# The last 128 rows of w2, four to a partition on 32 partitions, in a decode step of attention and a Mish layer

## The chip, the cores and the metric

The kernel runs on one core of a Trainium2 chip. The metric is device time in microseconds of one execution, the median of several; lower is better. All data is float32.

## The reference

Two branches work on the same input x (2 rows of 512) and are mixed by a gate. Branch A is one decode step of attention: 32 query heads over 8 key/value heads of width 128, a cache of which the last 4096 positions count, softmax, and an output projection wo. Branch B is a dense layer w1 (512 to 1792), Mish, and a dense layer w2 (1792 to 512).

```python
g = sigmoid((x * gate_w).sum(-1, keepdims=True))
q = (x @ wq) in heads                       # 32 heads of 128
p = softmax(q @ k^T * 128**-0.5)            # k, v: the last 4096 positions
a = (p @ v) in rows @ wo                    # [2, 4096] @ [4096, 512]
h = x @ w1 + b1                             # [2, 1792]
b = (h * tanh(softplus(h))) @ w2            # [2, 1792] @ [1792, 512]
return g * a + (1 - g) * b
```

## The kernel before

All weights and the cache are read once, 91 MB in all, by DMAs that the SP queue issues in the order of the code. Big loads go through a pool of five buffers (`stream`, L46 and L54 to L57): a load is issued when the buffer that it reuses is free. The order is wq (two loads, with the small vector `sm` between them), w1, then k and v of the eight key/value heads in turn, then `w2_0` (the first ten blocks of 128 rows of w2, L270), then wo in four pieces of 4, 2, 1 and 1 key/value heads (L271, here called wo0, wo4, wo6 and wo7), and at last the rest of w2 in pieces of two, one and one blocks (L272; `CUTS`, L39; here called w2_10, w2_12 and w2_13). The three last pieces have buffers of their own (pool `ends`), so they wait for nothing but their turn on SP. Each load fills all 128 partitions, and each partition's part is one run of memory.

Early on, `queries` (L112) projects x with wq, and `hidden` (L207) computes the Mish layer up to `actT`, whose column block f holds 128 activations of w2's row block f; (1 - g) is folded in. `hidden` brings four groups of 32 output rows from PSUM through ACT (L218, L219), transposes them with four TensorE transposes (L228), adds the bias on DVE (L232), and does the rest on POOL, ACT and DVE (L237 to L245).

Then for each key/value head come `softmax` (L131) and `values` (L150). After the last head, `outputs` (L199) puts the heads' results into `oT`.

The last matmuls are of two kinds. `project` (L278, matmul at L279) adds a product with 512 columns into one of four groups of 32 rows of `acc`; four of them, one a group, run beside each other. It takes the ten blocks of `w2_0` and the 32 heads of wo. When all of `acc` is there, ACT copies its first half and DVE its second half into `asum` (L307, L308). `finish` (L287, matmul at L289) adds products of four times 128 columns into the four groups of `fin`: `output(1)` for w2_10, then `asum` against `fold`, which adds up the four groups of `acc`, then `output(2)` for w2_12 and `output(3)` for w2_13. DVE copies `fin` (L320) and SP stores it (L321).

The framework orders each engine's instructions by its own estimate of when operands arrive; in the trace the last `outputs` (L201) runs ahead of the ten blocks of `w2_0`, though the code has it behind them. A float32 matmul is two instructions in the trace (each with its weight load), so that four matmuls, one for each group, are eight.

Of the kernel before, what the change touches and what calls it, by code (L numbers as in the profile page):

```python
# [8 lines left out]
F32 = mybir.dt.float32  # L9
AF = mybir.ActivationFunctionType  # L10
ALU = mybir.AluOpType
AX = mybir.AxisListType

P = 128
B = 2
D = 512
HQ = 32
HKV = 8
REP = HQ // HKV
# [5 lines left out]
NJ = 4  # L25
NT = 4
Q = 32
RS = Q // B
BH = B * REP
F = 1792  # L30
DC = D // P
FC = F // P
FG = 4
HALF = 4
CHUNK = 8192
SMALL = DC * B + DC + FC
SCALE = DH ** -0.5
CAP = 20.0
CUTS = (0, 10, 12, 13, 14)  # L39


@with_exitstack
def decode_kernel(ctx: ExitStack, tc: tile.TileContext, res, stored, small, wq, kt, v, wo, w1, w2, out):
    nc = tc.nc

    stream = ctx.enter_context(tc.tile_pool(name="stream", bufs=5))  # L46
    ends = ctx.enter_context(tc.tile_pool(name="ends", bufs=1))
# [39 lines left out]
    nc.gpsimd.memset(qz, 0.0)  # L87
    oT = const.tile([P, HQ, Q], F32, name="oT")
    nc.gpsimd.memset(oT, 0.0)
    actT = const.tile([P, FC, Q], F32, name="actT")  # L90
    nc.gpsimd.memset(actT, 0.0)
    mx = const.tile([P, HKV], F32, name="mx")
    ls = const.tile([P, HKV], F32, name="ls")
# [113 lines left out]
    def hidden(t):  # L207
        w = t[:, : DC * F].rearrange("p (c f) -> p c f", c=DC)
        hp = ps_1.tile([P, FG * P], F32, tag="o", name="hp")
        for c in range(DC):  # L210
            for j in range(NJ):
                n = min(FG, FC - j * FG) * P
                nc.tensor.matmul(hp[Q * j : Q * j + Q, :n], x32[:, c, :],  # L213
                                 w[:, c, j * FG * P : j * FG * P + n],
                                 start=(c == 0), stop=(c == DC - 1))
        hs = work.tile([P, FG * P], F32, tag="p", name="hs")
        nl = (FC - (NJ - 1) * FG) * P
        nc.scalar.copy(hs[:, :nl], hp[:, :nl])  # L218
        nc.scalar.copy(hs[: Q * (NJ - 1), nl:], hp[: Q * (NJ - 1), nl:])  # L219
        ht = ps_1.tile([P, FG, NJ, Q], F32, tag="pt", name="ht")  # L220

        def m(name):
            return const.tile([P, FC, B], F32, name=name)

        h, e, nu, de, ho = (m(x) for x in ("h", "e", "nu", "de", "ho"))
        for k in range(FG):
            nj = len(range(k, FC, FG))
            nc.tensor.transpose(ht[:, k, :nj, :].rearrange("p j r -> p (j r)"),  # L228
                                hs[: Q * nj, k * P : (k + 1) * P], ident[: Q * nj, : Q * nj])
        for j0, j1, nk in ((0, NJ - 1, FG), (NJ - 1, NJ, FC - (NJ - 1) * FG)):  # L230
            f0, f1 = j0 * FG, (j1 - 1) * FG + nk
            nc.vector.tensor_tensor(  # L232
                h[:, f0:f1, :].rearrange("p (j k) b -> p j k b", k=nk),
                ht[:, :nk, j0:j1, ::RS].rearrange("p k j b -> p j k b"),
                b1[:, f0:f1].rearrange("p (j k) -> p j k", k=nk)[:, :, :, None]
                .to_broadcast([P, j1 - j0, nk, B]), op=ALU.add)
        nc.gpsimd.tensor_scalar_min(e, h, CAP)  # L237
        nc.scalar.activation(e, e, AF.Exp)
        nc.gpsimd.tensor_tensor(ho, h, omg[:, None, :].to_broadcast([P, FC, B]), op=ALU.mult)
        nc.gpsimd.tensor_scalar_add(nu, e, 2.0)  # L240
        nc.gpsimd.tensor_tensor(nu, nu, e, op=ALU.mult)
        nc.gpsimd.tensor_scalar_add(de, nu, 2.0)
        nc.vector.reciprocal(de, de)
        nc.gpsimd.tensor_tensor(nu, nu, de, op=ALU.mult)
        nc.gpsimd.tensor_tensor(actT[:, :, ::RS], nu, ho, op=ALU.mult)  # L245
# [11 lines left out]
    def load_w2(i):  # L257
        f0, f1 = CUTS[i], CUTS[i + 1]
        src = w2[f0 * P * D : f1 * P * D].rearrange("(p x) -> p x", p=P)
        if i == 0:  # L260
            return load(src, (f1 - f0) * D, f"w2_{f0}")
        t = ends.tile([P, (f1 - f0) * D], F32, name=f"w2_{f0}")
        nc.sync.dma_start(t, src)
        return t

    def load_wo(k0, k1):
        return load(wo[k0 * REP * D * P : k1 * REP * D * P].rearrange("(p x) -> p x", p=P),
                    (k1 - k0) * REP * D, f"wo{k0}")

    w2_0 = load_w2(0)  # L270
    wos = [(k0, k1, load_wo(k0, k1)) for k0, k1 in ((0, 4), (4, 6), (6, 7), (7, 8))]  # L271
    tail = [load_w2(i) for i in range(1, len(CUTS) - 1)]  # L272

# [4 lines left out]
    def project(j, lhsT, rhs, n):  # L278
        nc.tensor.matmul(acc[Q * j : Q * j + Q, :], lhsT, rhs,  # L279
                         start=(n_col[j] == 0), stop=(n_col[j] == n - 1))  # L280
        n_col[j] += 1

    n_of = [HKV + len(range(j, CUTS[1], NJ)) for j in range(NJ)]
    n_fin = FC - CUTS[1] + 1
    done = [0]

    def finish(lhsT, rhs):  # L287
# [9 lines left out]
    values(HKV - 1, pT, last_v)  # L297
    for f in range(CUTS[1]):
        project(f % NJ, actT[:, f, :], w2_0[:, f * D : (f + 1) * D], n_of[f % NJ])
    outputs(ol, kf, r, HKV - 2, HKV)  # L300
    for k0, k1, t in wos:
        for kv in range(k0, k1):
# [7 lines left out]
    def output(i):  # L310
        for f in range(CUTS[i], CUTS[i + 1]):
            x = (f - CUTS[i]) * D
            finish(actT[:, f, :], tail[i - 1][:, x : x + D])
# [1 line left out]
    output(1)  # L315
    finish(fold, asum)
    output(2)
    output(3)

    copy = nc.vector.tensor_copy(res, fin)  # L320
    store = nc.sync.dma_start(out, res).then_inc(stored, 16)  # L321
# [51 lines left out]
```

## Time and profile before

| | |
|---|---|
| time, median of 3 runs | 219.93 us (219.87 to 219.94) |
| the profiled execution's own time | 219.96 us |
| its span, first to last instruction | 218.1 us |
| mean granted TensorE clock | 0.82 of full speed |
| read from memory, rate over the span | 91.24 MB, 419 GB/s |
| busy: PE, PEld, DVE, ACT, POOL | 128.1, 39.7, 22.1, 15.3, 7.5 us |

Between the span and the time of the same execution lie 1.86 us. Times within the profile are microseconds from the span's start. PE is the matmul side of TensorE, PEld its weight loads; SPq is SP's queue, from which the DMAs are issued. A DMA's share of 1.00 means that all 16 DMA engines of the core are at work.

### The profile page before, as it was taken

To read this page: it belongs to the slowest core of one execution; us is meant where nothing else is said; L and a number is where in the kernel's file an instruction comes from. 1 tells how busy PE (TensorE), PEld (TensorE's weight loads), DVE (VectorE), ACT (ScalarE), POOL (GpSimd) and SP (SyncE) were. 2 spreads that over 40 slices of the span, in tenths; PEclk is the share of its full clock that TensorE was granted. 3 is DMA by queue.
4 is the path that set the end of the run, shared out by engine and by line. 5 is a ranking of instruction groups with operands and counts; after the bars stand their busy time and mean duration, and the time that the engine had idled before them with its cause. 6 is when DMAs were issued, how large, how long until landed. Compare 5 with 4: busy or idle time off the path is not lost.

```text
span 218.1 us, 1832 instructions
## 1 busy us (share of the span) xinstructions
PE 128.1 (59%) x804; PEld 39.7 (18%) x804; DVE 22.1 (10%) x34; ACT 15.3 (7%) x34; POOL 7.5 (3%) x29
## 2 busy tenths in 40 slices
PE   0059855275565619555571944477293837593995
PEld 0023221012111202111120211112021212432222
DVE  0000000010001230100105010010501002105001
ACT  2000111001002000200200020011002001100000
POOL 7000002000000000000000000000000000100000
PEclk9999999578859985797967599676969797557599
DMA  7998999999999999999999999999999999999992
GB/s 288 409 459 385 452 413 472 391 475 403 463 415 451 412 451 415 451 415 451 421 442 427 433 433 439 427 439 424 439 427 445 421 445 404 436 449 427 406 408 109
DMA packets 4182, 91.41 MB, mean 419 GB/s; under 512 B 592, under 2 KB 720, under 8 KB 1104
## 3 DMA queue, kind: packets, MB, share of 16 engines
q1 hardware_dynamic: 4176, 91.31, 97.6%
q8 instruction: 6, 0.10, 0.2%
HBM read 91.24 MB, written 0.07 MB: 419 GB/s over the span
## 4 chain that ended last, share of the span: by engine, by line
DMA 82%; PE 14%; DVE 1%; SPq 1%; issue 1%; ACT 1%; POOL 0%; POOLq 0%
DMA k<-in_kt 41%; DMA w<-in_w 21%; DMA v<-in_v 19%; PE sc L135 5%; PE o L156 4%; PE hp L213 2%; PE ol L201 1%; PE fin L289 1%; SPq L56 1%; ACT p L140 0%; DVE mx L138 0%; PE lp L192 0%; POOL ms L180 0%; DVE r L195 0%; SPq L61 0%
## 5 line engine op out<-in xcount | busy, mean ns | idle before, releaser
L135 PE MATMUL sc<-k,qz 128*32 128x512 f32 x256 | 46.0, 885 | 40.1 <-DMA k<-in_kt 40.1
L156 PE MATMUL o<-v,pT 128*32 128x512 f32 x256 | 39.2, 768 | 11.4 <-DMA v<-in_v 11.4
L135 PEld LDWEIGHTS sc<-k,qz 128*32 128x32 f32 x256 | 10.3, 154 | 74.5 <-DMA k<-in_kt 46.7
L156 PEld LDWEIGHTS o<-v,pT 128*32 128x32 f32 x256 | 10.9, 136 | 34.1 <-issue 28.2
L138 DVE TENSOR_REDUCE mx<-sc 128x1 f32<-128x512 f32 x8 | 5.5, 692 | 107.1 <-PE sc L135 107.1
L117 PE MATMUL qp<-wqa,x 128*32 128x512 f32 x32 | 8.0, 953 | 13.4 <-POOL x L85 13.4
L140 ACT ACTIVATE p<-sc,mx 128x512 f32<-128x512 f32 x8 | 5.5, 687 | 131.8 <-DVE mx L138 131.8
L144 PE MATMUL pp<-ident,p 128*128 128x128 f32 x32 | 5.3, 287 | 12.1 <-ACT p L140 12.1
L279 PE MATMUL acc<-wo,oT 128*32 128x512 f32 x64 | 8.7, 616 | 0.4 <-DMA wo<-in_wo 0.4
L163 DVE TENSOR_TENSOR om<-o,pick 128x1024 f32<-128x1024 f32 x4 | 4.9, 1224 | 29.0 <-PE o L156 29.0
L166 DVE TENSOR_REDUCE od<-om 128x256 f32<-128x1024 f32 x4 | 7.5, 1884 | 0.1
L144 PEld LDWEIGHTS pp<-ident,p 128*128 128x128 f32 x32 | 3.4, 141 | 19.1 <-ACT p L140 19.1
L201 PE MATMUL ol<-kf,od 128*128 128x8 f32 x16 | 3.8, 364 | 3.9 <-DVE od L166 3.3
L180 POOL TENSOR_TENSOR ms<-ms,top 8x64 f32<-8x64 f32 x2 | 0.6, 310 | 146.4 <-DVE top L178 146.4
L145 ACT COPY pT<-pp 128x512 f32<-128x512 f32 x8 | 4.7, 586 | 6.2 <-PE pp L144 6.2
L279 PE MATMUL acc<-w,actT 128*32 128x512 f32 x20 | 5.1, 1037 | 0.0
L213 PE MATMUL hp<-w,x 128*32 128x512 f32 (+1 forms) x32 | 3.6, 542 | 1.9 <-DMA w<-in_w 1.9
L117 PEld LDWEIGHTS qp<-wqa,x 128*32 128x32 f32 x32 | 1.5, 157 | 17.3 <-POOL x L85 13.4
L201 PEld LDWEIGHTS ol<-kf,od 128*128 128x128 f32 x16 | 3.6, 328 | 5.0 <-DVE od L166 4.2
L117 PE MATMUL qp<-wqb,x 128*32 128x512 f32 x32 | 3.6, 595 | 0.0
L279 PEld LDWEIGHTS acc<-wo,oT 128*32 128x32 f32 x64 | 2.2, 113 | 5.9 <-issue 4.7
L307 ACT COPY asum<-acc 128x256 f32<-128x256 f32 x1 | 0.4, 372 | 27.7 <-PE acc L279 27.7
(67 smaller groups left out, 33.0 us busy)
## 6 DMA issues: line engine op xcount, KB each, us to landing
k<-in_kt SPq DMA_DIRECT2D x8, 4096.0 KB, 43.1
v<-in_v SPq DMA_DIRECT2D x8, 4096.0 KB, 42.6
wqa<-in_wq SPq DMA_DIRECT2D x1, 4096.0 KB, 12.2
wqb<-in_wq SPq DMA_DIRECT2D x1, 4096.0 KB, 21.1
wo<-in_wo SPq DMA_DIRECT2D x1, 4096.0 KB, 39.3
w<-in_w SPq DMA_DIRECT2D x1, 3584.0 KB, 29.1
w<-in_w SPq DMA_DIRECT2D x1, 2560.0 KB, 39.5
wo<-in_wo SPq DMA_DIRECT2D x1, 2048.0 KB, 34.4
```

What stands on the lines that cost most here:

```text
L117: nc.tensor.matmul(qp[Q * k : Q * k + Q, :], x32[:, c, :], w[:, c, k, :], start=(c == 0), stop=(c == DC - 1))
L135: nc.tensor.matmul(sc[Q * j : Q * j + Q, :], qz[:, kv, m * Q : m * Q + Q], t[:, (m * NJ + j) * 512 : (m * NJ + j + 1) * 512], start=(m == ...
L138: nc.vector.tensor_reduce(mx[:, kv : kv + 1], sc, axis=AX.X, op=ALU.max, negate=True)
L140: nc.scalar.activation(p, sc, AF.Exp, bias=mx[:, kv : kv + 1], accum_out=ls[:, kv : kv + 1])
L144: nc.tensor.transpose(pp[:, c, :], p[:, c * P : (c + 1) * P], ident)
L145: nc.scalar.copy(pT, pp)
L156: nc.tensor.matmul(o[Q * j : Q * j + Q], pT[:, c, Q * j : Q * j + Q], t[:, (c * NJ + j) * 512 : (c * NJ + j + 1) * 512], start=(c == 0), s ...
L163: nc.vector.tensor_tensor(ov, pair[0].rearrange("p k (m d) -> p k m d", m=BN), pick[:, None, :, None].to_broadcast([P, 2, BN, DH]), op=ALU ...
L166: nc.vector.tensor_reduce(od[:, kv - 1 : kv + 1], ov.rearrange("p k m d -> p k d m"), axis=AX.X, op=ALU.add)
L201: nc.tensor.matmul(ol[:, kv].rearrange("p b h -> p (b h)"), od[:, kv, :], kf[:, kv, :], start=True, stop=True)
L213: nc.tensor.matmul(hp[Q * j : Q * j + Q, :n], x32[:, c, :], w[:, c, j * FG * P : j * FG * P + n], start=(c == 0), stop=(c == DC - 1))
L279: nc.tensor.matmul(acc[Q * j : Q * j + Q, :], lhsT, rhs, start=(n_col[j] == 0), stop=(n_col[j] == n - 1))
```

## The change

The 14th block of w2 (rows 1664 to 1791) leaves the tail. It is laid out as four rows of w2 per partition on partitions 0 to 31, 8 KB a partition (`w2_x`), and loaded right behind `w2_0` by four DMAs, the i-th of which fills partitions i, i+4, ..., i+28. It is used by four matmuls with 32 rows instead of 128, one for each group of `acc`, placed behind the ten blocks of `w2_0`; `output(3)` is gone. For these matmuls the last 128 activations must lie as four columns of 32 partitions: `hidden` gets four more transposes of 32 columns each, into a PSUM tile `hx` of their own, one more bias add, and a memset of `h`; `actT` and the Mish tiles grow from 14 to 17 columns. The vector `sm` grows by three columns.

```diff
+FM = FC - 1
+NX = P // Q
+FA = FM + NX
-SMALL = DC * B + DC + FC
+SMALL = DC * B + DC + FA
-CUTS = (0, 10, 12, 13, 14)
+CUTS = (0, 10, 12, 13)
...
-    actT = const.tile([P, FC, Q], F32, name="actT")
+    actT = const.tile([P, FA, Q], F32, name="actT")
...
-            return const.tile([P, FC, B], F32, name=name)
+            return const.tile([P, FA, B], F32, name=name)
...
         for k in range(FG):
-            nj = len(range(k, FC, FG))
+            nj = len(range(k, FM, FG))
             nc.tensor.transpose(ht[:, k, :nj, :].rearrange("p j r -> p (j r)"),
                                 hs[: Q * nj, k * P : (k + 1) * P], ident[: Q * nj, : Q * nj])
-        for j0, j1, nk in ((0, NJ - 1, FG), (NJ - 1, NJ, FC - (NJ - 1) * FG)):
+        jx, kx = FM // FG, FM % FG
+        hx = ps_1.tile([P, NX, NJ, Q], F32, tag="q", name="hx")
+        for q in range(NX):
+            nc.tensor.transpose(hx[:Q, q].rearrange("p j r -> p (j r)"),
+                                hs[:, kx * P + q * Q : kx * P + (q + 1) * Q], ident)
+        nc.gpsimd.memset(h, 0.0)
+        nc.vector.tensor_tensor(h[:Q, FM:, :], hx[:Q, :, jx, ::RS],
+                                b1[:Q, FM:, None].to_broadcast([Q, NX, B]), op=ALU.add)
+        for j0, j1, nk in ((0, NJ - 1, FG), (NJ - 1, NJ, FM - (NJ - 1) * FG)):
...
     w2_0 = load_w2(0)
+    w2_x = ends.tile([P, NX * D], F32, name="w2_x")
+    for i in range(REP):
+        nc.sync.dma_start(w2_x[i:Q:REP, :], w2x[i])
     wos = [(k0, k1, load_wo(k0, k1)) for k0, k1 in ((0, 4), (4, 6), (6, 7), (7, 8))]
...
-    n_of = [HKV + len(range(j, CUTS[1], NJ)) for j in range(NJ)]
-    n_fin = FC - CUTS[1] + 1
+    n_of = [HKV + len(range(j, CUTS[1], NJ)) + 1 for j in range(NJ)]
+    n_fin = FM - CUTS[1] + 1
...
     for f in range(CUTS[1]):
         project(f % NJ, actT[:, f, :], w2_0[:, f * D : (f + 1) * D], n_of[f % NJ])
+    for q in range(NX):
+        project(q, actT[:Q, FM + q, :], w2_x[:Q, q * D : (q + 1) * D], n_of[q])
     outputs(ol, kf, r, HKV - 2, HKV)
...
     finish(fold, asum)
     output(2)
-    output(3)
...
+    w2x = a("B_w2")[FM * P :].reshape(NX, Q // REP, REP, D).transpose(2, 1, 0, 3)
```

## Rows read from the trace of the kernel before

**Rows 1.** The page: DMA share and rate in forty slices, and the chain's shares.

```profile
DMA  7998999999999999999999999999999999999992
GB/s 288 409 459 385 452 413 472 391 475 403 463 415 451 412 451 415 451 415 451 421 442 427 433 433 439 427 439 424 439 427 445 421 445 404 436 449 427 406 408 109
DMA 82%; PE 14%; DVE 1%; SPq 1%; issue 1%; ACT 1%; POOL 0%; POOLq 0%
```

**Rows 2.** The chain that ended last, its end: start, length, what.

```profile
197.84 16.40 DMA w<-in_w
...
214.29 1.78 PE fin L289 x40
...
216.09 0.29 DVE res L320
```

**Rows 3.** The timeline of the tail: start, length, instruction, idle time before it.

```profile
213.07 1.06 PE L279 MATMUL acc<-wo,oT 128*32 128x512 f32 x8 [0.36 <-DMA wo<-in_wo]
214.21 0.37 ACT L307 COPY asum<-acc 128x256 f32<-128x256 f32 x1 [27.67 <-PE acc L279]
...
214.29 0.65 PE L289 MATMUL fin<-w,actT 128*32 128x128 f32 x16
214.61 0.42 DVE L308 COPY asum<-acc 128x256 f32<-128x256 f32 x1 [12.70 <-ACT asum L307]
...
215.10 0.30 PE L289 MATMUL fin<-w,actT 128*32 128x128 f32 x2
...
215.24 0.79 PE L289 MATMUL fin<-w,actT 128*32 128x128 f32 x14
```

**Rows 4.** The busy times by stretch, around the end of the DMAs.

```profile
core 0: us, PE busy (x) PEld busy (x) DVE busy (x) ACT busy (x) POOL busy (x), PEclk, DMA share, GB/s
...
213.00:213.20 0.20, 0.13 (x4) 0.13 (x8) 0.00 (x0) 0.00 (x0) 0.00 (x0) 1.00 1.03 410
...
213.60:214.00 0.40, 0.40 (x8) 0.00 (x0) 0.00 (x0) 0.00 (x0) 0.00 (x0) 1.00 0.38 149
...
214.60:214.80 0.20, 0.20 (x15) 0.20 (x8) 0.19 (x1) 0.00 (x0) 0.00 (x0) 1.00 0.34 133
...
215.00:215.20 0.20, 0.20 (x8) 0.11 (x8) 0.04 (x1) 0.00 (x0) 0.00 (x0) 1.00 0.11 41
```

**Rows 5.** The page: DMA queues and kinds, with packets, MB and share.

```profile
q1 hardware_dynamic: 4176, 91.31, 97.6%
q8 instruction: 6, 0.10, 0.2%
```

**Rows 6.** The timeline of SP's queue: the last loads before the store.

```profile
154.01 0.33 SPq L56 DMA_DIRECT2D w<-in_w  x1
...
197.84 1.37 SPq L263 DMA_DIRECT2D w<-in_w  x3
```

**Rows 7.** The issue and landing of the loads at L263.

```profile
L263 SPq DMA_DIRECT2D w<-in_w x3: 423/427/432, 197.8 to 198.8; - x3
DMA to landing us min/median/max: 16.4/16.6/16.8
```

**Rows 8.** The busy times by stretch, from the last head's values to wo7.

```profile
197.40:200.60 3.20, 0.00 (x0) 0.00 (x0) 3.10 (x2) 0.00 (x0) 0.00 (x0) 0.83 1.07 461
200.60:206.30 5.70, 5.63 (x28) 2.08 (x30) 0.20 (x2) 0.00 (x0) 0.00 (x0) 0.50 0.93 398
206.30:212.70 6.40, 6.40 (x56) 1.71 (x50) 0.00 (x0) 0.00 (x0) 0.00 (x0) 1.00 0.99 413
```

**Rows 9.** The timeline of TensorE between the last outputs and wo7.

```profile
200.67 1.02 PE L201 MATMUL ol<-kf,od 128*128 128x8 f32 x4 [3.28 <-DVE od L166]
...
201.62 4.48 PE L279 MATMUL acc<-w,actT 128*32 128x512 f32 x18
...
202.48 0.20 PEld L279 LDWEIGHTS acc<-w,actT 128*32 128x32 f32 x4 [0.66 <-issue]
203.33 0.20 PEld L279 LDWEIGHTS acc<-w,actT 128*32 128x32 f32 x4 [0.66 <-issue]
...
206.54 0.15 PEld L279 LDWEIGHTS acc<-wo,oT 128*32 128x32 f32 x6 [0.47 <-issue]
...
207.40 0.15 PEld L279 LDWEIGHTS acc<-wo,oT 128*32 128x32 f32 x6 [0.32 <-issue]
```

**Rows 10.** The instructions of L279 that read wo: shortest, median, longest in ns.

```profile
L279 PE MATMUL acc<-wo,oT x64: 592/592/1062, 205.0 to 213.5; 128*32 128x512 f32 x64
```

**Rows 11.** The timeline around the Mish layer, and POOL's next work after it.

```profile
35.51 0.65 PE L228 MATMUL ht<-ident,hs 128*128 128x128 f32 x4 [0.55 <-ACT hs L218]
...
38.92 0.25 POOL L245 TENSOR_TENSOR actT<-nu,ho 128x28 f32<-128x28 f32 x1
...
42.42 3.63 PE L135 MATMUL sc<-k,qz 128*32 128x512 f32 x16 [6.25 <-DMA k<-in_kt]
...
185.61 0.59 POOL L180 TENSOR_TENSOR ms<-ms,top 8x64 f32<-8x64 f32 x2 [146.44 <-DVE top L178]
```

**Rows 12.** The page: the issue of w2_0, KB, us to landing.

```profile
w<-in_w SPq DMA_DIRECT2D x1, 2560.0 KB, 39.5
```

More of the change, by code (lines that the diff above doesn't have):

```diff
@@ L33, with decode_kernel @@
 FG = 4
+FM = FC - 1
+NX = P // Q
+FA = FM + NX
 HALF = 4
 CHUNK = 8192
-SMALL = DC * B + DC + FC
+SMALL = DC * B + DC + FA
 SCALE = DH ** -0.5
 CAP = 20.0
-CUTS = (0, 10, 12, 13, 14)
+CUTS = (0, 10, 12, 13)
 @with_exitstack
-def decode_kernel(ctx: ExitStack, tc: tile.TileContext, res, stored, small, wq, kt, v, wo, w1, w2, out):
+def decode_kernel(ctx: ExitStack, tc: tile.TileContext, res, stored, small, wq, kt, v, wo, w1, w2, w2x, out):
     nc = tc.nc
@@ L238, in hidden @@
         nc.scalar.activation(e, e, AF.Exp)
-        nc.gpsimd.tensor_tensor(ho, h, omg[:, None, :].to_broadcast([P, FC, B]), op=ALU.mult)
+        nc.gpsimd.tensor_tensor(ho, h, omg[:, None, :].to_broadcast([P, FA, B]), op=ALU.mult)
         nc.gpsimd.tensor_scalar_add(nu, e, 2.0)
@@ L337 @@
     x = a("A_x")[:, 0, :]
+    b1 = a("B_b1")
     small = np.concatenate([
@@ L340 @@
         a("gate_w").reshape(DC, P).T,
-        a("B_b1").reshape(FC, P).T,
+        b1[: FM * P].reshape(FM, P).T,
+        np.concatenate([b1[FM * P :].reshape(NX, Q).T, np.zeros((P - Q, NX), b1.dtype)]),
     ], axis=1)
@@ L358 @@
         "w2": c(w2),
+        "w2x": c(w2x.reshape(REP, Q // REP, NX * D)),
     }
```

## The prediction

> **What bounds the kernel now.** I read the page's slices and chain first. All but the first and the last slices have the DMA engines busy nine tenths or more of the time, and DMAs make up 82% of the chain that ended last [rows 1]. So the stream of loads sets the pace, and since the change reads the same bytes, only its end can move: what lands last, and what must still run after that. For this the end of the chain, then the timeline of the tail.
>
> The chain's last DMA is w2_10: issued at 197.84, landed 16.40 later at 214.24. Then `fin` takes 1.78 us and DVE copies the result from 216.09 [rows 2]. The timeline shows a second line beside it. wo7's eight instructions start at 213.07, on their DMA's landing, and run 1.06 us. ACT's half of `asum` starts at 214.21, DVE's at 214.61 and ends at 215.03. The `fin` work behind it starts at 215.10, and the last of it ends at 216.03 [rows 3]. w2_13 is issued last of the three at L263; 198.8 and the longest landing, 16.8, give 215.6 [rows 7]. So three things end close together: w2_10 at 214.24, `asum` at 215.03, w2_13 at about 215.6.
>
> The stretches show how the loads run out. The DMA share is 1.03 up to 213.2, then 0.38 at 213.6 to 214.0, 0.34 at 214.6 and 0.11 at 215.0 [rows 4]. A share of 0.38 is six engines of sixteen: ten are done at about 213.5, six work on for some 1.3 us. The page shows six packets of kind "instruction", 0.10 MB in all, 16 KB each [rows 5]. Six late engines and six such packets: I read each fetch as having put one engine, a different one each time, behind the rest. The trace doesn't number the engines; whether they are among those that the change loads more is the question on which the forecast hangs.
>
> **The change, part by part.**
>
> *Taken from the tail.* w2_13's eight `fin` instructions go. What is then last is `asum`: DVE ends at 215.03 and `fin` goes on at 215.10. The four groups' passes follow each other at 0.117 us (sixteen instructions in 0.65, the first 0.30 long, so three steps in 0.35). Left are two passes of the second half of `fold` and two of w2_12: 215.10 + 3 x 0.117 + 0.30 = 215.75 instead of 216.03 [rows 3]. Gain: 0.28, taken as 0.3. That w2_13's landing moves from 215.6 gives no more than this, because `asum` doesn't move with it.
>
> *Added to TensorE.* Four matmuls of 512 columns, eight instructions. No row has one with 32 rows and 512 columns; the nearest are the same shape with 128 rows. Eight of these take 0.86 at the full clock (207.40 less 206.54) and 1.70 at half (203.33 less 202.48 is 0.85 for four) [rows 9]. The ends are nothing, if the four run in an idle time, and 1.70. They need `w2_x`, which follows `w2_0`, and the trace has the blocks of `w2_0` behind the last `outputs` at 201.62 [rows 9], although TensorE idles from 197.4 to 200.6 [rows 8]. I assume the same order. [...] The clock rises at its time, so the price is a round at the full clock, 0.86. Of this the idle time before wo7 takes 0.36 [rows 3], and the pipelined end another 0.16: a pass is shown 592 ns long [rows 10], but the next starts 0.43 after it. 0.86 - 0.52 = 0.34. So wo7 starts about 0.3 later than 213.07, and with it `asum` and the end. Cost: 0.3.
>
> *Moved among the loads.* 256 KB that were last now come ahead of wo0, wo4, wo6, wo7, w2_10 and w2_12, and the bytes in front of each are 256 KB more. At 413 GB/s [rows 8] this is 0.63 us if all engines share it evenly. Do they? 4176 packets on the loads' queue [rows 5] are 29 DMAs (28 loads and the store) of 128 rows and 16 more each, so a row is a packet, and a DMA of eight rows can use eight engines at most. Four such DMAs of 8 KB rows put 32 KB on each if they all go to the same eight: at 413/16 = 25.8 GB/s an engine, 1.25 us for these and none for the others. The ten engines that are early have 1.3 us to spare, so loads on them land no later than the late six do now. So the landing of wo7 stays if the eight are clear of the six, and moves by 1.25 if any of the six is among them.
>
> [...]
>
> *Costed at nothing.* The Mish layer's four more transposes, its memset, its bias add and its wider tiles: the whole of L228 to L245 takes from 35.51 to 39.17, TensorE's next work waits for k until 42.42 [rows 11], and `actT` isn't used before 201.62. Four transposes now take 0.65, so four more fit five times into the gap of TensorE. POOL has nothing else to do until 185.61 [rows 11], and DVE's next reduction waits for TensorE. Without this cover they would cost about 1 us: 0.65 of transposes and some 0.3 for the bias add. SP's four more issues take 0.43 each, 1.7 in all, by those at L263 [rows 7]; they come after 154.01, and the blocks that they deliver are used at 201.62 [rows 6, 9]. They are queued ahead of wo's issues, but a load issued at that place lands 39.5 us later [rows 12], nearly all of it in the queue, so 1.7 later on SP is nothing. The tail's issues start at 197.84 as before, behind wo7's.
>
> *The sum*, against the profiled execution's own 219.96: -0.3 + 0.3 = 0.0. The median is 0.03 lower, so 219.93.
>
> **The rivals.**
>
> *The eight engines hold at least one of the late six.* Place: wo7. Its landing is that of its slowest engine, so it moves by 1.25, to 213.07 + 1.25 = 214.32; TensorE's extra round, over by 213.4, is hidden. Less the 0.3 of w2_13: 219.93 + 0.95 = 220.9. One late engine among the eight is enough. For it: a set of eight out of sixteen hardly misses six by chance. [...] I weigh this as a judgement, without a row that decides.
>
> *The load is shared evenly*, the four DMAs going to different engines: wo7 lands 0.63 later, at 213.70, past TensorE's 213.4. 219.93 + 0.63 - 0.3 = 220.26.
>
> *TensorE takes the four matmuls in its idle time at 197.4 to 200.6*, by another order. Then their cost of 0.3 is gone, and the end is `asum` at the old 215.03: 219.63. If the clock also stays up through 206.3, wo7 still waits for its DMA at 213.07, so no more comes of it. For it: w2_0 and w2_x land well before. Against it: the order that the trace shows.
>
> *A change of the array's shape empties TensorE*, going into the 32-row matmuls and out of them. The trace has the change from 128*128 to 128*32 at 201.62, before the 128*128 work's end at 201.69 [rows 9], and so shows no emptying. As a mechanism of this kernel, two times the 0.16 by which a pass outlasts the next one's start: 219.93 + 0.32 = 220.25. [...]
>
> **How the numbers follow.** Eight clear of six, as forecast: 0.46, at 219.93, its own range 219.6 to 220.3 (the four matmuls at nothing or at another order's full 0.86). Late engines among the eight: 0.27, 220.9. Idle time used: 0.12, 219.63. Even split: 0.08, 220.26. Emptying: 0.05, 220.25. The rest, 0.02, is something faster that I don't see. The range goes from 219.6 to 221.0; of the first and third cases a part lies below it. A measurement of this kernel can tell about 0.2%, 0.44 us, from no change. Slower than 220.37: 0.27 and 0.05 from the upper ends of the even split, the emptying and the forecast, 0.32. Faster than 219.49: 0.03 of the forecast, 0.05 of the idle time, 0.02 of the rest, 0.10. Same: 0.58.
>
> **What the profile afterwards would show.** Right: w2_10 lands near 214.2 and wo7's matmuls start near 213.4, on TensorE and not on a DMA; `asum`'s second half ends near 215.3; TensorE's L279 stretch is eight instructions longer; the DMA share at the end no longer has a long step near 0.38. Late engines among the eight: wo7's matmuls wait for their DMA until about 214.3, and few engines work alone to the end. Even split: wo7 at 213.7, the step at 0.38 as long as now. Idle time used: L279 in 197.4 to 200.6. Wrong altogether: a stretch before 193 that is longer than now, or L201 or L279 waiting for `w2_x`.

## The result, and the profile after

| | before | after |
|---|---|---|
| median of 22 runs each, in turns on one chip | 220.10 us (219.78 to 220.67) | 220.61 us (219.43 to 221.59) |
| ratio after to before | | 1.0025, 95% from 1.0013 to 1.0037 |
| profiled execution, its span | 219.96, 218.1 | 220.56, 218.7 |
| wo7's matmuls start | 213.07 | 214.00 |
| w2_10 has landed (`fin` starts) | 214.29 | 215.24 |
| `asum`'s second half starts on DVE | 214.61 | 215.54 |
| the result is copied | 216.09 | 216.70 |

The changed kernel is slower by a quarter of a per cent, 0.5 us. The forecast was 219.93, no change. The single times after fall into groups: three at 219.43 to 219.66, one at 220.02, eleven at 220.44 to 220.85 and seven at 221.37 to 221.59; those of before fill 219.78 to 220.67. The profiled execution belongs to the group that holds the median.

The page after, its rows on DMA rate, chain and queues, beside [rows 1, 5]:

```profile
GB/s 282 390 476 390 451 412 470 402 461 414 455 419 443 416 443 431 431 437 425 437 422 455 408 455 408 461 402 464 396 461 402 464 396 445 419 472 393 423 408 75
DMA 81%; PE 12%; another core or an unknown queue 3%; DVE 1%; SPq 1%; ACT 1%; issue 1%; POOL 0%; POOLq 0%
q1 hardware_dynamic: 4096, 91.31, 97.3%
q8 instruction: 6, 0.10, 0.2%
```

The stream runs as before up to its end, and there are again six instruction fetches. The packets tell how the new loads are spread: 28 DMAs (27 loads and the store) of 128 rows with 16 more packets each are 4032, and 64 are left for the four of eight rows, 8 and 8 each. By the sizes in the trace these are eight of 8 KB and eight of 4 bytes, where a DMA of 128 rows has sixteen of 4 bytes (480 of them in all; 464 before).

The end of the chain, beside [rows 2], and the timeline of the tail, beside [rows 3] (start, length, instruction, idle time before it):

```profile
196.58 18.61 DMA w<-in_w
...
215.24 1.44 PE fin L303 x32
...
216.70 0.29 DVE res L335
```

```profile
211.65 1.06 PE L293 MATMUL acc<-wo,oT 128*32 128x512 f32 x8 [0.62 <-DMA wo<-in_wo]
...
214.00 1.06 PE L293 MATMUL acc<-wo,oT 128*32 128x512 f32 x8 [1.29 <-DMA wo<-in_wo]
215.13 0.37 ACT L323 COPY asum<-acc 128x256 f32<-128x256 f32 x1 [28.98 <-PE acc L293]
...
215.54 0.43 DVE L324 COPY asum<-acc 128x256 f32<-128x256 f32 x1 [15.24 <-ACT asum L323]
...
216.17 0.48 PE L303 MATMUL fin<-w,actT 128*32 128x128 f32 x6
```

wo7 waits 1.29 us for its DMA and starts 0.93 later than before; w2_10 lands 0.95 later. Only the last step came nearer: 32 `fin` instructions in 1.44 where 40 took 1.78. So + 0.93 or 0.95 from the loads, - 0.3 from the shorter `fin`, gives + 0.6, which is what the two profiled executions differ by (220.56 and 219.96).

How the loads run out, by stretch (busy time of each engine, then the granted clock, the DMA share and the rate), beside [rows 4]:

```profile
core 0: us, PE busy (x) PEld busy (x) DVE busy (x) ACT busy (x) POOL busy (x), PEclk, DMA share, GB/s
213.80:214.20 0.40, 0.20 (x4) 0.16 (x8) 0.00 (x0) 0.00 (x0) 0.00 (x0) 1.00 0.58 225
214.20:214.60 0.40, 0.40 (x8) 0.00 (x0) 0.00 (x0) 0.00 (x0) 0.00 (x0) 1.00 0.27 108
214.60:215.00 0.40, 0.40 (x8) 0.00 (x0) 0.00 (x0) 0.00 (x0) 0.00 (x0) 1.00 0.12 46
```

Before, the step was 0.38, six engines of sixteen. Now it is 0.58, nine or ten engines, and then 0.12, two engines alone. This is the count that two late engines among the eight give: of the eight loaded ones, six have only the load's delay; of the six late ones, four have only the fetch's; both delays are somewhat over a microsecond (about 1.1 and 1.2 by the middles of the ranges in the table below), so ten engines work on and stop one after the other up to about 214.5; two have both delays and end last.

The shares alone don't tell one engine from another, and no view numbers them, but the trace keeps the start, length and size of every packet. In the running stream a packet mostly starts 3 or 4 ns before the one ahead of it on the same engine ends. Followed that way from 26 us on, the packets of the loads fall into sixteen chains, one an engine, without another gap than these: six chains have one break each, of 0.86 to 0.94 us, just behind a fetch. Each of the four 8-row DMAs has its eight packets in the same eight chains. The last packets of the loads end, by kind of chain:

| | before | after |
|---|---|---|
| no fetch, no 8-row packets | ten, 213.28 to 213.63 | four, 212.88 to 213.39 |
| 8-row packets alone | | six, 213.96 to 214.44 |
| a fetch alone | six, 214.72 to 215.24 | four, 214.17 to 214.54 |
| both | | two, 215.49 and 215.50 |

So the count holds engine by engine, and so does the prediction's reading that each fetch had put a different engine behind.

SP's queue, beside [rows 6], and TensorE around the new matmuls, beside [rows 9]:

```profile
154.59 4.58 SPq L284 DMA_DIRECT2D w_x<-in_w2x  x4
168.25 28.28 SPq L59 DMA_DIRECT2D wo<-in_wo  x4
196.58 0.90 SPq L274 DMA_DIRECT2D w<-in_w  x2
```

```profile
200.00 4.33 PE L293 MATMUL acc<-w,actT 128*32 128x512 f32 x20
...
204.26 0.20 PEld L293 LDWEIGHTS acc<-w_x,actT 32*32 32x32 f32 x8 [1.67 <-issue]
204.26 1.14 PE L293 MATMUL acc<-w_x,actT 32*32 32x512 f32 x8
205.33 0.16 PEld L293 LDWEIGHTS acc<-wo,oT 128*32 128x32 f32 x8 [0.88 <-issue]
```

The four issues are over long before their blocks are used, and wo's matmuls stand directly behind the 32-row ones. From 205.33 on TensorE waits for the loads twice, 0.62 us in front of wo6 and 1.29 in front of wo7; its extra round is not what this execution ends on.

### The profile page after: what moved, and what is told of

It is laid out like the page before. It is cut to its first block, busy times and chain, and to the rows that moved or that the text cites. A ratio compares the mean times of both kernels' runs of the same rounds, so it can differ in the third digit from the quotient of the medians.

```text
span 218.7 us, 1848 instructions
## 1 busy us (share of the span) xinstructions
PE 129.8 (59%) x808; PEld 39.1 (18%) x808; DVE 22.5 (10%) x35; ACT 15.3 (7%) x34; POOL 7.8 (4%) x30
## 4 chain that ended last, share of the span: by engine, by line
DMA 81%; PE 12%; another core or an unknown queue 3%; DVE 1%; SPq 1%; ACT 1%; issue 1%; POOL 0%; POOLq 0%
DMA k<-in_kt 39%; DMA w<-in_w 22%; DMA v<-in_v 20%; PE o L159 5%; PE sc L138 5%; PE ol L204 1%; PE fin L303 1%; SPq L59 1%; ACT p L143 0%; DVE mx L141 0%; POOL ms L183 0%; DVE r L198 0%; PE lp L195 0%; SPq L64 0%
## 5 line engine op out<-in xcount | busy, mean ns | idle before, releaser
L138 PE MATMUL sc<-k,qz 128*32 128x512 f32 x256 | 41.7, 812 | 32.2 <-DMA k<-in_kt 32.2
L159 PE MATMUL o<-v,pT 128*32 128x512 f32 x256 | 43.2, 836 | 15.4 <-DMA v<-in_v 15.4
L138 PEld LDWEIGHTS sc<-k,qz 128*32 128x32 f32 x256 | 9.6, 143 | 64.5 <-DMA k<-in_kt 39.7
L159 PEld LDWEIGHTS o<-v,pT 128*32 128x32 f32 x256 | 11.5, 145 | 40.6 <-issue 37.6
L120 PE MATMUL qp<-wqa,x 128*32 128x512 f32 x32 | 7.0, 819 | 13.6 <-POOL x L88 13.6
L293 PE MATMUL acc<-wo,oT 128*32 128x512 f32 x64 | 7.7, 598 | 2.0 <-DMA wo<-in_wo 1.9
L216 PE MATMUL hp<-w,x 128*32 128x512 f32 (+1 forms) x32 | 6.4, 893 | 2.9 <-DMA w<-in_w 2.9
L293 PE MATMUL acc<-w,actT 128*32 128x512 f32 x20 | 4.3, 840 | 0.0
L293 PEld LDWEIGHTS acc<-wo,oT 128*32 128x32 f32 x64 | 1.7, 109 | 8.0 <-issue 4.8
L216 PEld LDWEIGHTS hp<-w,x 128*32 128x32 f32 x32 | 1.7, 163 | 6.7 <-issue 6.7
```

The source lines that it names most:

```text
L120: nc.tensor.matmul(qp[Q * k : Q * k + Q, :], x32[:, c, :], w[:, c, k, :], start=(c == 0), stop=(c == DC - 1))
L138: nc.tensor.matmul(sc[Q * j : Q * j + Q, :], qz[:, kv, m * Q : m * Q + Q], t[:, (m * NJ + j) * 512 : (m * NJ + j + 1) * 512], start=(m == ...
L159: nc.tensor.matmul(o[Q * j : Q * j + Q], pT[:, c, Q * j : Q * j + Q], t[:, (c * NJ + j) * 512 : (c * NJ + j + 1) * 512], start=(c == 0), s ...
L216: nc.tensor.matmul(hp[Q * j : Q * j + Q, :n], x32[:, c, :], w[:, c, j * FG * P : j * FG * P + n], start=(c == 0), stop=(c == DC - 1))
L293: nc.tensor.matmul(acc[Q * j : Q * j + Q, :], lhsT, rhs, start=(n_col[j] == 0), stop=(n_col[j] == n - 1))
```

## The experiments

Two theories stood after the result. **A, the loads:** the four DMAs use the same eight engines, two of which also carry a fetch, and these two bring wo7 and w2_10 about a microsecond later. **B, TensorE:** the extra round and the change of the array's shape in and out of it move wo's matmuls, and wo7's wait is an accident of the profiled execution. All medians below are beside the kernel before in the same series: 220.06 (15 runs) in the first, 219.94 (35) in the second, 219.93 (22) in the last.

**The change again.** As it is, timed in the first series.

> The changed kernel as it is, for its spread and a second trace. Theory A (lopsided load): the four DMAs of eight rows put 32 KB on the same eight DMA engines, and the six instruction fetches fall on other engines in each execution, so the time moves in steps with how many late engines lie among the eight: single times between 219.4 and 221.6, far more spread than the kernel before (219.8 to 220.7). The number of engines that still work alone at the end of the loads need not be the two of the first trace. Theory B (TensorE): the four more matmuls and two changes of the array's shape make it slower by a fixed amount; the spread is then that of the granted clock's phase, and the low single times are those with the higher mean clock.

Measured: 220.78 (220.55 to 221.02, five runs), ratio 1.0034 (1.0021 to 1.0046). In its trace wo7 starts at 214.24 behind its DMA, and the DMA share from 214.6 to 215.0 is 0.14. The loss and its picture repeat; the wide spread that theory A expected doesn't show in these five runs.

**The loads alone.**

```diff
-    n_of = [HKV + len(range(j, CUTS[1], NJ)) + 1 for j in range(NJ)]
+    n_of = [HKV + len(range(j, CUTS[1], NJ)) for j in range(NJ)]
...
-    for q in range(NX):
-        project(q, actT[:Q, FM + q, :], w2_x[:Q, q * D : (q + 1) * D], n_of[q])
```

> The change without its four 32-row matmuls: w2's last block is loaded but its product is left out of the output. Theory A: the loads set the end, so nothing is gained where a late engine lies among the eight: median 220.5, single times up to about 221.3. Theory B: TensorE's round and the two shape changes are gone and the tail is eight instructions shorter than before: 219.6 to 219.8, narrow.

Measured: 220.52, ratio 1.0006 (0.9992 to 1.0021), but no run lies near the middle of its range: five are at 219.61 to 219.80 and six at 220.52 to 220.75. The upper six have the whole loss without one 32-row matmul. The trace is of the lower group (219.8); by stretch, the timeline of wo's matmuls, and the chain's end:

```profile
213.60:214.00 0.40, 0.40 (x8) 0.00 (x0) 0.00 (x0) 0.00 (x0) 0.00 (x0) 1.00 0.82 318
214.00:214.40 0.40, 0.38 (x8) 0.11 (x8) 0.00 (x0) 0.05 (x1) 0.00 (x0) 1.00 0.39 149
214.40:214.80 0.40, 0.40 (x18) 0.29 (x17) 0.04 (x1) 0.32 (x1) 0.00 (x0) 1.00 0.03 10
```

```profile
210.67 3.60 PE L293 MATMUL acc<-wo,oT 128*32 128x512 f32 x28
```

```profile
214.73 0.02 issue
214.76 0.44 DVE asum L322
...
215.24 0.66 PE fin L303 x12
215.91 0.29 DVE res L333
```

Here the share is 0.82, thirteen engines, then 0.39 while they stop one after the other, and from 214.4 next to nothing: eight loaded and six late are fourteen, and none has both delays. The chains of packets say the same: two without either delay end at 212.96 and 213.13, eight with 8-row packets at 213.83 to 214.28, six with a fetch at 214.29 to 214.60. wo7 has landed by the time TensorE reaches it (no wait in 210.67 to 214.27), and the chain ends by `asum` and the shorter `fin`, as the forecast had it. So the same loads cost a microsecond at the end or nothing, by whether the late engines are among the eight, and that differs from one execution to the next.

**The change, traced four more times,** to catch the groups of its times. The kernel is the changed one as it is.

> The changed kernel once more, for a trace of another execution. Theory A: the time follows from how many late engines lie among the eight that carry the four DMAs of eight rows. At about 219.5 the loads end with none of them (the landing of w2_12 near 214.9, and a DMA share near 0.4 up to it); at about 220.6 one to three engines work alone for 1.2 to 1.3 at the end (share 0.06 to 0.19) and w2_12 lands near 215.9.

Measured: 220.64, 220.55, 220.47 and 220.53, all of the middle group. wo7's matmuls start at 214.09, 214.00, 213.92 and 213.98, each behind its DMA, and w2_10's `fin` at 215.32, 215.23, 215.15 and 215.21. The last packets of the loads end at 215.41 to 215.59, where 215.9 was expected. The fourth's stretches:

```profile
213.40:213.80 0.40, 0.00 (x0) 0.00 (x0) 0.00 (x0) 0.00 (x0) 0.00 (x0) 1.00 0.70 277
213.80:214.20 0.40, 0.22 (x4) 0.16 (x8) 0.00 (x0) 0.00 (x0) 0.00 (x0) 1.00 0.52 200
214.20:214.60 0.40, 0.40 (x8) 0.00 (x0) 0.00 (x0) 0.00 (x0) 0.00 (x0) 1.00 0.22 87
```

TensorE does nothing from 213.4 to 213.8, at the full clock, and waits. The mean clocks of the four were 0.828, 0.813, 0.828 and 0.852, and the times don't follow them. What was expected for the lowest and the highest group stays untried, since none of the four fell into them.

**The matmuls alone,** added to the kernel before, with 32 rows and with 128.

```diff
-    n_of = [HKV + len(range(j, CUTS[1], NJ)) for j in range(NJ)]
+    n_of = [HKV + len(range(j, CUTS[1], NJ)) + 1 for j in range(NJ)]
...
+    for q in range(NJ):
+        project(q, actT[:Q, q, :], w2_0[:Q, q * D : (q + 1) * D], n_of[q])
```

> The kernel before, with four more matmuls of 32 rows behind the ten blocks of w2_0 (they read the first 32 rows of w2_0 and their product goes into the sum, which is no part of the reference). No load is changed. Theory A (lopsided load and travelling fetches): the loads are those of before, so nothing but the extra round less its slack: 220.1 to 220.5, no steps. Theory B (TensorE sets the end, by the phase of its clock): executions in which the clock is low between the last values and wo7 go up by the whole round and its two shape changes, 0.9 to 1.5, others by nothing: median 220.6, single times from 219.9 to 221.5, as the changed kernel has.

The other reads `actT[:P, ...]` and `w2_0[:P, ...]` instead.

> As the run with 32 rows, but with four extra matmuls of 128 rows, so that the array's shape doesn't change (their product is no part of the reference either). If the shape change costs two times 0.16 or more, this is 0.2 to 0.4 below the run with 32 rows; if it costs nothing, the two are equal.

Measured: with 32 rows 220.27, ratio 1.0021 (1.0002 to 1.0040), twelve runs in groups (five at 219.72 to 219.91, two near 220.27, three at 220.75 to 220.88, two at 221.75 to 221.80). With 128 rows 220.07, ratio 1.0006 (0.9991 to 1.0022). The two intervals overlap, so the shape's own price is not settled by them. With 32 rows the median lies where theory A had it, but the steps are those that A had ruled out; the spread is B's, with a lower median. The trace with 32 rows, of the 220.8 group, TensorE's timeline and two stretches:

```profile
201.89 6.20 PE L279 MATMUL acc<-w,actT 128*32 128x512 f32 x28
208.02 7.07 PE L279 MATMUL acc<-wo,oT 128*32 128x512 f32 x64
```

```profile
200.90:206.30 5.40, 5.37 (x24) 1.89 (x24) 0.18 (x1) 0.00 (x0) 0.00 (x0) 0.50 0.98 419
206.30:214.90 8.60, 8.60 (x76) 2.26 (x76) 0.00 (x0) 0.00 (x0) 0.00 (x0) 0.97 0.89 367
```

wo's 64 instructions run without a wait for a DMA and end at 215.09; with the loads of before, TensorE is the bound. At the granted clock 0.50 for 5.4 us it has no time left: it is busy for 5.37 of these 5.40 and for all of the 8.60 behind them. So B's mechanism exists, and its price at the median is 0.33, about the forecast's 0.34 (only two of the twelve times lie there, between the groups); what it does in the changed kernel, where wo7 lands a microsecond later, is the next pair's question.

**Another order,** the last `outputs` behind w2_0's and the new matmuls, in both kernels, by a dependency without a semaphore. The edit of the changed kernel (the kernel before has the same without the 32-row matmuls):

```diff
+            if behind is not None:
+                tc.add_manual_dep(mm.ins, behind.ins.name, mybir.DependencyInfo(
+                    mybir.DependencyClass.NoSync, mybir.DependencyReason.DATA), reason="order")
...
-        project(q, actT[:Q, FM + q, :], w2_x[:Q, q * D : (q + 1) * D], n_of[q])
-    outputs(ol, kf, r, HKV - 2, HKV)
+        last = project(q, actT[:Q, FM + q, :], w2_x[:Q, q * D : (q + 1) * D], n_of[q])
+    outputs(ol, kf, r, HKV - 2, HKV, last)
```

> The changed kernel, with the last outputs' matmuls put behind the blocks of w2_0 and the four 32-row matmuls, so that these run while DVE makes od. Theory A: the loads set the end, so single times stay in two groups, 219.4 to 219.7 (no late engine among the eight) and 220.4 to 220.7 (some), median 220.5; the group at 221.4 is gone only as far as it was TensorE's. Theory B: all of the loss is gone, 219.6, narrow.

> The kernel before with the same order. Its end is w2_13's landing and 0.5 of work behind it in the traced execution, so there is nothing to gain there: 219.9. If its slower single times (220.4 to 220.7) are TensorE's, they go, and the median falls from 220.06 to 219.8 to 219.9.

Measured: the change with this order 220.67, ratio 1.0032 (1.0019 to 1.0045), ten of twelve runs at 220.55 to 220.92. Before with this order 219.90 (219.77 to 220.05), ratio 0.9996 (0.9988 to 1.0005). TensorE's timeline of the change with this order:

```profile
197.59 2.74 PE L296 MATMUL acc<-w,actT 128*32 128x512 f32 x20
200.26 1.06 PE L296 MATMUL acc<-w_x,actT 32*32 32x512 f32 x8
201.25 0.61 PE L204 MATMUL ol<-kf,od 128*128 128x8 f32 x4
204.30 6.80 PE L296 MATMUL acc<-wo,oT 128*32 128x512 f32 x48 [2.44 <-DMA wo<-in_wo]
...
214.06 1.07 PE L296 MATMUL acc<-wo,oT 128*32 128x512 f32 x8 [1.29 <-DMA wo<-in_wo]
```

All the new TensorE work is over at 201.3, wo's first piece waits 2.44 for its load, and wo7 starts at 214.06 all the same. With TensorE out of the way the loss is whole: the median's loss is the loads'. In the kernel before, the same order takes away the upper single times (the highest of eleven is 220.05, where nine of 35 lay above that, up to 220.75) and next to nothing from the median: by this those upper times were TensorE's, as far as eleven runs can tell.

**One DMA for the 32 partitions instead of four.** The rows lie four in a partition, next to each other, so one load takes partitions 0 to 31. By its page it has 48 packets (4080 less 28 times 144), one for each partition and sixteen more, as a DMA of 128 rows has; I take it from this to use all sixteen engines.

```diff
-    for i in range(REP):
-        nc.sync.dma_start(w2_x[i:Q:REP, :], w2x[i])
+    nc.sync.dma_start(w2_x[:Q, :], w2x)
```

> One DMA of all 32 partitions in place of the four, so that all sixteen engines share the 256 KB; the rest of the change stays. Theory A: wo7 lands later by 0.63 in every execution, whichever engines the fetches fall on: about 220.2 to 220.4, with the spread of the kernel before, no single time above 220.9. Theory B: as the changed kernel, 220.6, with the same spread up to 221.6.

Measured: 221.74 (221.70 to 221.97, five runs), ratio 1.0080 (1.0067 to 1.0092). This was a miss, by over a microsecond. The page's DMA rate in its 40 slices, and TensorE's timeline:

```profile
GB/s 286 411 449 412 453 427 420 453 405 459 399 470 399 461 417 441 435 423 453 405 461 393 470 399 459 423 432 447 417 447 411 456 399 446 414 337 441 411 407 66
```

```profile
208.18 1.06 PE L292 MATMUL acc<-w_x,actT 32*32 32x512 f32 x8
209.17 7.30 PE L292 MATMUL acc<-wo,oT 128*32 128x512 f32 x64
216.63 0.64 PE L302 MATMUL fin<-w,actT 128*32 128x128 f32 x16 [0.16 <-DMA w<-in_w]
```

In slice 36, 192.6 to 198.1, the rate is 337; after has nothing below 390 between its first and last slice. Against some 430 that is 93 GB/s for 5.5 us, 0.51 MB or 1.2 us of stream. That comes on top of the 0.63 that the bytes themselves take. The packets show where it goes: of the 32 KB packets, which usually take 1.21 us, 27 that start between 191.9 and 195.2 take 1.46 to 2.34 us. Why they take longer no run shows; the four DMAs write the same partitions from eight engines without such a dip (390 or more in the page after).

TensorE was late in the traced execution as well (wo from 209.17), but it ends on the loads: `fin` starts behind w2_10's landing at 216.63, 2.34 later than before, and 219.96 + 2.34 - 0.34 is 221.96, where this execution took 221.97. Of the 2.34, the dip and the bytes give 1.8; what the rest is stays open.

**The even load, without the 32 partitions:** before, with its last block loaded early in the old layout of 128 partitions, and one matmul of 128 rows into the third group.

```diff
-CUTS = (0, 10, 12, 13, 14)
+CUTS = (0, 10, 12, 13)
...
+    w2_x = ends.tile([P, D], F32, name="w2_x")
+    nc.sync.dma_start(w2_x, w2[FM * P * D :].rearrange("(p x) -> p x", p=P))
...
+    project(2, actT[:, FM, :], w2_x, n_of[2])
```

> The kernel before with its last block of w2 loaded as early as in the change, but in the old layout: one DMA over 128 partitions and one matmul of 128 rows into the third group of acc. [...] By theory A wo7 lands 0.63 later than before in every execution and w2_13's 0.3 falls away: 220.1 to 220.4, one group. If moving the bytes ahead of wo7 were itself the cost of the change, it would be 220.6.

Measured: 220.25 (220.09 to 220.45, eleven runs, one group), ratio 1.0012 (1.0003 to 1.0021). TensorE's timeline, and a stretch of the loads' end:

```profile
211.52 1.06 PE L282 MATMUL acc<-wo,oT 128*32 128x512 f32 x8 [0.60 <-DMA wo<-in_wo]
213.88 1.07 PE L282 MATMUL acc<-wo,oT 128*32 128x512 f32 x8 [1.30 <-DMA wo<-in_wo]
```

```profile
214.20:214.60 0.40, 0.40 (x8) 0.00 (x0) 0.00 (x0) 0.00 (x0) 0.00 (x0) 1.00 0.34 133
```

Shared evenly, the 256 KB still stand in front of wo7, which starts 0.81 later than 213.07 (0.63 had been worked out), and the end keeps its step of six engines, 0.34. (The traced execution is the slowest of the eleven.) It loses 0.3 at the median and 0.16 to 0.52 in single runs, where the four DMAs lose 0.5 at the median and gain in some. So an early place costs 0.3 even with an even load; the rest of the change's loss is the load on eight engines.

**The four DMAs twice,** to double the load on the eight engines.

```diff
+    for i in range(REP):
+        nc.sync.dma_start(w2_0[i:Q:REP, 6144:], w2x[i])
```

> The change with the four DMAs issued twice (the second copy goes to an unused part of the tile of w2_0): 64 KB more on each of the engines that carry them. Theory A: if the four go to the same eight engines, wo7 lands another 1.25 later in each execution: median about 221.9. If they are shared evenly, another 0.63. Theory B: no change against the changed kernel, 220.6.

Measured: 224.16 (223.96 to 225.63, five runs), ratio 1.0216 (1.0187 to 1.0244), nearly three times the highest price expected, and by something else. SP's queue, and what it waited for (us in total, times, longest):

```profile
152.78 6.09 SPq L284 DMA_DIRECT2D w_x<-in_w2x  x4
167.91 26.05 SPq L286 DMA_DIRECT2D w<-in_w2x  x4
194.07 2.99 SPq L59 DMA_DIRECT2D wo<-in_wo  x4
```

```profile
SPq L286 <- DMA v<-in_v: 18.0, 2, 9.0
SPq L286 <- DMA k<-in_kt: 9.1, 1, 9.1
SPq L286 <- DMA w<-in_w: 5.4, 1, 5.4
```

The second four issues wait, one after the other, for the landing of older loads; three of these are loads of `k` and `v` that have nothing to do with their bytes. wo's four issues, queued behind them, come at 194.07 instead of 168.25 and on. The stream then ran thin (294 GB/s in slice 35 of its page). What ties the second four to these loads no run shows. As a measure of the eight engines this run is worth nothing.

**Which part makes the highest group?** Seven of 22 runs of the change were at 221.37 to 221.59. Two kernels: the loads alone with eight more early transposes, for a count of instructions nearer to the change's; and the change with its 32-row matmuls twice.

```diff
-        for q in range(NX):
+        for q in 3 * list(range(NX)):
```

> The changed kernel without its four 32-row matmuls (their product is left out of the output), and with eight more of the small transposes early in the Mish layer, so that TensorE has as many instructions as in the changed kernel but no more work at the end. If the group of single times at 221.4 to 221.8 comes from TensorE's extra round at the end, it is absent: two groups, 219.6 to 219.8 and 220.5 to 220.8. If it comes from the number of instructions (another fetch, or one at another time), it is there, in about one execution of four.

```diff
-    for q in range(NX):
+    for q in 2 * list(range(NX)):
```

> The changed kernel with its four 32-row matmuls done twice, so that w2's last block counts twice in the output. If TensorE's extra round makes the upper group, a second round of 0.86 to 1.7 makes it more frequent and higher (above half of the executions over 221.2, some near 222.5 to 223.2). If the loads alone set the time, nothing moves: median 220.6.

Measured: the loads alone with more transposes 220.62 (220.49 to 220.82, five runs), none in the highest group, nor in the lowest. The matmuls twice 220.61, ratio 1.0021 (1.0005 to 1.0037): three of eleven at 219.49 to 219.74, six at 220.46 to 220.77, two at 221.06 and 221.21. That is a miss for what was expected if TensorE caused that group: a second round made it neither higher nor more frequent. TensorE's timeline of the latter:

```profile
206.03 1.92 PE L293 MATMUL acc<-w_x,actT 32*32 32x512 f32 x16
207.88 7.23 PE L293 MATMUL acc<-wo,oT 128*32 128x512 f32 x64
215.26 0.64 PE L303 MATMUL fin<-w,actT 128*32 128x128 f32 x16
```

Here two rounds of 32 rows stand on TensorE, and wo's matmuls end at 215.11, within 0.05 of where the changed kernel's end behind their DMA (214.00 + 1.06). The last eight start 0.55 behind the ones ahead of them (213.50 and 214.05), where 0.43 is the step, so wo7's wait is down to about 0.1: in this execution the late load just covers the second round too.

What makes the times above 221.3 stays open. They came in the change (7 of 22, and none of the nine later runs), and once or twice in three kernels with four more matmuls behind w2_0 (2 of 12, 1 of 12, 1 of 12). Two of these three have the loads of before, so the group needs no late load. They didn't come in before, nor in the kernels without those matmuls or with one more, nor, quite, with eight. No trace caught one. The miss doesn't rule TensorE out. In the trace of the loads alone with more transposes the last `outputs` start at 201.95 (199.46 to 200.24 in the six traces of the change), w2_0's blocks at 202.90, and the granted clock is 0.50 up to 207.6. With a round of 32 rows behind these blocks wo7 would start near 202.90 + 5.18 + 0.99 + 6.02 = 215.09 (5.18 is what the blocks take in the trace of the change again, there too at 0.50 but for the end; 6.02 is seven rounds of 0.86), 1.09 later than in the change's trace, and the time would be about 221.6. That is an estimate, and it doesn't fit the one time of 221.74 with the other order, where the round is off the path.

## Why the prediction was wrong, point by point

**The bound** was read rightly: the stream sets the pace, 81% of the chain after, and the change acts at its end only.

**w2_13's `fin`:** - 0.28 forecast. The last step is 1.44 instead of 1.78, and the end moved 0.61 where the landings moved 0.93 and 0.95, so about - 0.3. Right.

**The loads** are where it failed. The forecast named the question, whether the eight engines are clear of the six late ones, gave each answer its price, and chose "clear" by a judgement "without a row that decides". In nine of ten traces of the change and of the kernels with its four DMAs in one set, two engines work alone at the end and both delays fall together; in one, of the loads alone, none does. So wo7's landing, which the forecast left in place, came later in all six traces of the change, and TensorE's round, which it had put on the path, was hidden behind that. In the timed runs of the change three or four of 22 are of the low kind. The price of that answer was close: wo7 by 1.25 forecast, by 0.85 to 1.17 in six traces of the change (213.92 to 214.24 less 213.07), so that the time came out at 220.6 rather than 220.9. What was sized right and weighted wrong was the case. The prediction's own sentence, that eight of sixteen hardly miss six, had a number it didn't work out: of the 12870 ways to choose eight engines 45 leave out a given six. Only an order among the engines could make "clear" likely, and no row showed one. Without such a row the rival deserved most of the chance.

That it was two engines or none in these ten traces, and never three or four, need not be a chance pick either. The breaks in the chains of packets show an order. In order of time, in ns, those of chains with 8-row packets marked with a star:

| trace | the six breaks |
|---|---|
| before | 950, 932, 863, 864, 924, 915 |
| the change | 861\*, 864\*, 919, 915, 903, 943 |
| the change again | 946, 933, 862\*, 868\*, 918, 914 |
| matmuls twice | 907, 950, 945, 931, 861\*, 863\* |
| the loads alone | 918, 915, 906, 943, 942, 929 |

I read them as one round of eight engines, entered at different places, of which two neighbours (about 860 to 870) are among the eight with 8-row packets; all ten traces fit it, and the five above enter it at four places, each two from the next. Six fetches an execution are two short of a round, so by this reading the entry moves by two, and the two neighbours are both met or both left out: left out from one entry of four. This is worked out from the lengths of the breaks and no run tests it. If the four entries come equally often, "clear" had a chance of a quarter (an estimate), not 0.46, and not the 45 in 12870 either; the single times have it in 3 of 22 with the change and 5 of 11 with the loads alone.

**The spread over eight engines.** That the four DMAs go to the same eight, and the 0.08 for the even split, were the author's estimate: no row of before has a DMA of eight rows. The runs showed the same eight: each DMA has its 8 and 8 packets, the chains of packets put all four on the same eight engines, and the shares agree: fourteen engines, or ten and then two, where an even spread leaves the old step of six, as the 128-partition load does (0.34).

**TensorE's round:** 0.34 forecast on the path. Alone, in the kernel before, its price at the median is 0.33, which is near by luck in part: the single times lie in groups at nothing, 0.9 and 1.8 with few between. In the change it is covered by wo7's wait and costs the median nothing, which the order experiment shows. That the clock rises at its time, which the price of a full-clock round uses, no run shows as a rule. Granted were 0.50 from 200.9 to 206.3 and 0.97 from there to 214.9 with the round in the kernel before; in the change 0.63 from 200.0 to 204.2, 0.88 up to 205.4 and 1.00 from there to 211.6. The condition was right (with wo7 landing a microsecond late the round is hidden, said the rival), but the forecast's case wasn't the one that happened. In the low group the change as is runs at 219.43 to 219.66, below 219.93 by 0.3 to 0.5; by the loads alone it is 219.61 to 219.80. So even there the round didn't show, though no trace of the change fell into that group to say why.

**The change of shape** goes with an emptied TensorE in these runs, other than [rows 9] had suggested for 128*128 to 128*32. In the run with the other order, at clock 1.00, the third round of w2_0 has work for two of the four groups only, and the 32-row matmuls start when it is through (2.67 after the start, three rounds of 0.86 and a little), although two of them are for the other two groups. With 128 rows these groups do run ahead: that trace has two instructions of wo at 204.23, before the last two of w2_0 at 205.00. And the next work starts 0.99 after the 32-row ones, where a round takes 0.86. It costs nothing in the end, for the reason above.

**The work costed at nothing** cost nothing that shows: the stream up to 190 runs as before. The four issues took 4.58 us on SP, not 1.7 (0.62 to 0.76 each instead of 0.43, and a wait of 1.8 for a landing of `k` among them), and pushed wo's issues back, but all loads were still queued far ahead. The doubled version shows that this cover has an end.

**The other rivals.** The even split was not what happened; built for itself, over 128 partitions, it gave 220.25, for which 220.26 had been worked out. TensorE's idle time wasn't used by the order that came out, and would have brought nothing: with that order forced the ratio is 1.0032.

No version beat both kernels. Before with the other order ties with it (0.9996, from 0.9988 to 1.0005), with a narrower spread.

## What to carry to other kernels

Here a DMA of eight rows loaded eight engines of sixteen. Before moving bytes ahead of a load that the end waits for, count the engines in the steps of the DMA share at the end (share times sixteen) and ask which of them the new bytes meet. The starts and lengths of the packets tell one engine from another even where no view numbers them, and the lengths of the breaks can show an order; if nothing tells, give the collision most of the chance. Bytes that were moved from last to early were not free here even when spread evenly, because wo7 with its work behind it moved back by them: 256 KB cost wo7 0.8 us and saved 0.3 us of `fin`. And the small DMAs had a price on the issuing queue, 0.62 to 0.76 us each where other loads took 0.33 or 0.43. It showed only when the queue ran out of its lead, with eight of them and wo's issues at 194.07.

## What the runs showed of the hardware that was not expected

- With 256 KB in one DMA to partitions 0 to 31 the stream fell to 337 GB/s for a slice of 5.5 us, and 32 KB packets of other loads there took up to 2.34 us instead of 1.21; with eight engines writing the same bytes, every fourth partition at a time, it stayed at 390 or more.
- The four 8-row DMAs used the same eight engines, and a fetch of 16 KB left a break of 0.86 to 0.95 us in one engine's packets. The lengths of the breaks can be read as one round over eight engines, two of which are among the eight. Whether they were met differed between traced executions, and single times of the same kernel lie about 0.9 us apart (219.61 to 219.80 and 220.52 to 220.75 with the loads alone).
- An 8-row DMA of every fourth partition took 0.62 to 0.76 us to issue where the other loads took 0.33 or 0.43 (0.88 for the one over 128 partitions), and four more of them held the queue for 26 us behind the landings of older loads.
- Four 32-row matmuls of 512 columns that came between 128-row ones took 0.99 us at the granted clock 1.00 until the next work started, where four of 128 rows took 0.86.
